# Late expert tiles: the store and the DMA transpose of half the inner layer move from SP's queue to ScalarE's, and the transpose moves behind turn_h

## The chip, the core and the metric

The kernel runs on one core of one Trainium2 chip. The metric is the device time of one execution in microseconds. The core has five engines that run their own instruction streams in order: TensorE (PE; PEld are its weight loads), VectorE (DVE), ScalarE (ACT), GpSimd (POOL) and SyncE (SP), which in this kernel issues nearly all plain DMA transfers.

## The reference

Attention with rotary embedding over 4 batches, 8 heads, 576 tokens and head size 64 is followed by a mixture of 8 experts. A token takes a fresh expert when its local gate is under 0.5, otherwise it keeps that of the token before it.

```python
x = attn_out.transpose(0, 2, 1, 3).reshape(B, S, 512)
...
for s in range(S):
    e = fresh_e if s == 0 or local_gate[b, s] < 0.5 else prev_e
    h = np.maximum(x[b, s] @ w1[e], 0.0)       # 512 -> 1024, the inner layer
    out[b, s] = p[e] * (h @ w2[e])             # 1024 -> 512
```

## The kernel before

The first part (to about 280 us) is attention and routing. The tokens are then sorted by expert into tiles of 128, and the experts run tile by tile: tiles 0 to 5 are the early ones, 6 to 18 the late ones, and tile 18 is the last. Float32 products are made of three passes over split numbers (a high part and the rest, `PASSES`). The change touches the late tiles alone, and there only tiles 6 to 17 (`by_dma`).

For each tile `first_product` makes the inner layer `h` in PSUM: 4 steps of 6 matmuls. `second_product` of the tile before it runs in between: 4 steps of 6 matmuls on the transposed, split inner layer `hs` (8 blocks of 128). A step of it reads two of the eight blocks of `hs`; the first two steps read blocks 0 to 3, the last two blocks 4 to 7.

The inner layer has to be transposed between the two products. Of tiles 6 to 17 the first half goes through TensorE: ScalarE applies the Relu (L943), `turn_h` transposes four blocks (L967), ScalarE copies the high part (L303) and VectorE makes the rest (L307). The second half goes through DRAM: VectorE copies it out of PSUM as two 16-bit planes (L942), a DMA stores the planes to `inner_d` (L944), and a DMA transpose brings them back as `ht` (L951, in `land_h`). One tile later `split_landed` makes the high part with Relu on ScalarE (L957) and the rest on VectorE (L958). The DMA transpose waits for the store's landing.

The weights of a tile are 8 chunks of 1024 columns, in four pairs A, B, C and D. They are loaded to the buffer `stage` by SP and split into a high part and the rest by `split_w`. Both happen only where the tile's expert differs from that of the tile before it; for late tiles each engine jumps over its share otherwise (L884 is that branch). For a late tile, of the splits of A (chunks 0 and 1) the high parts are on POOL (L877) and the rests on VectorE (L878). Of B, C and D, ScalarE makes the high parts of chunks 2, 5, 6 and 7 (L875), and POOL both parts of chunk 4. `load_pair(t + 1, c)` (L838) follows each split in SP's order. Where experts change from one tile to the next can be seen in the profile by the L875, L877 and L878 work: the new weights of tiles 11, 13 and 18 are split in late tiles, A and B during the tile before, C and D during the tile itself.

The order on every engine is the order in which the program is written; no scheduler moves anything in the late tiles. It is a string with one letter for each act:

```python
TILE = "ffAgffHfxBTssshsCDs"
```

`f` is a step of the first product, the fifth `f` takes the inner layer out of PSUM (L942, L943) and issues the store (L944). `x` transposes the next tile's tokens, `A` to `D` are the weight splits, `s` is a step of the second product, and the fifth `s` scales its result on ScalarE (`os`, L981) and issues POOL's scatter to the output (L982). `g` is POOL's gather of token rows (L908), `h` is `turn_h`, `T` is `land_h` and `H` is `split_landed` of the tile before.

Of the kernel before, what the change touches and what calls it, by code (L numbers as in the profile page):

```python
# [46 lines left out]
SPREAD_LAST = 127  # L47

TILE_EARLY = ("ffAffsfxBssgCsshD", "ffAffxfsBsCsgsshD", "fffAffxBssChsgssD", "ffAfffxBsssshsCDg", "ffAfffBsssxsshCgD", "fffxAffsBssgssChD")
TILE = "ffAgffHfxBTssshsCDs"  # L50
TILE_LAST = "ffxAffHfssBsChsDss"
PULL = 3
PE_LAG = 2
# [84 lines left out]
def tile_attention_moe(ctx, tc, qk, v, tabs, turn, consts, tri, wg, wts, out):  # L138
    nc = tc.nc
    pe, act, dve, pool, sp = nc.tensor, nc.scalar, nc.vector, nc.gpsimd, nc.sync  # L140
# [31 lines left out]
    inner_d = [dram.tile([P, 2, 512], U16, name=f"inner_{i}") for i in range(2)]  # L172
# [754 lines left out]
    def first_product(t):  # L927
        ps = ps_s.tile([P, 2, 512], F32, tag="s", name=f"h_{t}")
        for k in range(4):
            w = w_t.pop((t, k))  # L930
            for n, (x, y) in enumerate(PASSES):
                for c in range(2):
                    pe.matmul(ps[:, c], xs_t[t][:, x, k], w[y][:, c * 512:(c + 1) * 512],  # L933
                              start=(k == 0 and n == 0), stop=(k == 3 and n == 2))
            yield k
        h = ej_p.tile([P, 2, S], F32, tag="ej", name=f"hr_{t}").rearrange("p a s -> p (a s)")[:, 0:1024]
        h_t[t] = h
        if not by_dma(t):
            act.activation(h, ps.rearrange("p c n -> p (c n)"), AF.Relu)
            return  # L940
        planes = h[:, 512:].bitcast(U16).rearrange("p (l n) -> p l n", l=2)
        dve.tensor_copy(planes, ps[:, 1].bitcast(U16).rearrange("p (n l) -> p l n", l=2))  # L942
        act.activation(h[:, 0:512], ps[:, 0], AF.Relu)  # L943
        sp.dma_start(inner_d[t % 2], planes)  # L944

    def by_dma(t):
        return KE <= t < LAST

    def land_h(t):
        x = pk_p.tile([P, S], F32, tag="pk", name=f"ht_{t}")[:, 0:512]  # L950
        sp.dma_start_transpose(  # L951
            x.bitcast(U16).rearrange("p (k n) -> p k n", k=4), inner_d[t % 2].rearrange("t l n -> (t l) n"))
        landed[t] = x.rearrange("p (k n) -> p k n", k=4)

# [16 lines left out]
    def second_product(t):  # L971
        ps = ps_t.tile([P, 512], F32, tag="t", name=f"o_{t}")
        for k in range(8):
            w = w_t[t, 4 + k // 2]
            for n, (x, y) in enumerate(PASSES):
                pe.matmul(ps, hs_t[t][:, x, k], w[y][:, (k % 2) * 512:(k % 2 + 1) * 512],  # L976
                          start=(k == 0 and n == 0), stop=(k == 7 and n == 2))
            if k % 2 == 1:
                yield k
        o = et_p.tile([P, S], F32, tag="et", name=f"os_{t}")  # L980
        act.activation(o[:, 0:DM], ps, AF.Copy, scale=x_t[t][:, DM:DM + 1])  # L981
        done = pool.indirect_dma_start(  # L982
            out=outf, out_offset=bass.IndirectOffsetOnAxis(ap=sidx[:, t:t + 1], axis=0),
            in_=o[:, 0:DM], in_offset=None, bounds_check=NT - 1, oob_is_err=False)

        tc.declare_no_dep(done.ins, group="rows out", reason="rows of their own")
        tc.add_to_no_dep_group("rows out", done.ins)
# [3 lines left out]
    def experts_phase():  # L991
        for t in range(LAST + 1):
            first = first_product(t)
            second = second_product(t - 1) if t > 0 else iter(())
            for c in TILE_LAST if t == LAST else TILE if t >= KE else TILE_EARLY[t]:
                if c == "f":
# [10 lines left out]
                elif c == "s":  # L1007
                    if next(second, None) is not None:
                        yield t
                elif c == "x" and t < LAST:  # L1010
                    turn_x(t + 1)
                elif c in "AB" and t < LAST:
                    split_w(t + 1, "AB".index(c))
                elif c in "CD" and t > 0:
                    split_w(t, 2 + "CD".index(c))
                elif c == "h":
                    turn_h(t)
                    yield t + 1
                elif c == "T":
                    land_h(t)  # L1020
                elif c == "H" and by_dma(t - 1):
                    split_landed(t - 1)
                elif c == "g":
                    if t == 0:
                        gather(4)
                        gather(5)
                    elif KE < t + 2 <= LAST:
                        gather(t + 2)
# [3 lines left out]
    def rest_phase():  # L1032

        nl = nc.values_load_multi_w_load_instructions(meta[0:1, 60:61], min_val=U_LATE - 1, max_val=NLATE)[1][0]  # L1034

        def rest(t):
            with tc.If(nl > t - KE):
                expert_of(t)
                for k in range(8):
                    load_w(t, k)  # L1040
                regs.pop(t)
                gather(t)
                turn_x(t)
                for c in range(4):
                    split_w(t, c)
                list(first_product(t))
                turn_h(t)
                list(second_product(t))
                if t + 1 < NTILE:
                    rest(t + 1)  # L1050

        if LAST + 1 < NTILE:
            rest(LAST + 1)
# [294 lines left out]
```

## Time and profile before

| | |
|---|---|
| median of 3 runs | 549.62 us (549.24 to 551.68) |
| the profiled execution | 548.69 us, its span 546.8 us |
| PE busy | 520.2 us, 95% of the span |
| VectorE busy | 401.7 us, 73% |
| ScalarE busy | 334.1 us, 61% |
| POOL busy | 327.6 us, 60% |
| stores L944, DMA transposes L951 | 12 and 12, all on SP |

The span runs from the first to the last instruction. A row of the timeline gives the start in us, the time in us, engine, line, operation, what it writes and reads, the count, and in brackets how long the engine was idle before it and what ended that. "ACTq" and the like are the sequencers of the engines, with which branches and DMA issues are done. Rows of matmuls are modelled, so that neighbours can overlap a little.

### The profile page before, as it was taken

How to read it: one execution, taken by the hardware profiler on the slowest of the kernel's cores; microseconds unless marked ns; L12 is line 12 of the kernel's file. 1: busy time of each engine (PE TensorE's matmuls, PEld its weight loads, DVE VectorE, ACT ScalarE, POOL GpSimd, SP SyncE). 2: the span in 40 equal slices, each digit the busy share in tenths (PEclk: the TensorE clock that was granted, in tenths of full speed). 3: DMA queues.
4: the chain of work that ended last, by engine and by line, in shares of the span. 5: the costliest groups of instructions: out<-in, count | busy, mean ns of one | idle time of the engine just before them, and what ended most of it. 6: DMA issues, size and time to landing. Idle time of an engine off the chain costs nothing. (4 is left out here: it accounts for less than half of the span.)

```text
span 546.8 us, 10672 instructions
## 1 busy us (share of the span) xinstructions
PE 520.2 (95%) x3280; PEld 459.5 (84%) x3281; DVE 401.7 (73%) x736; ACT 334.1 (61%) x754; POOL 327.6 (60%) x243
## 2 busy tenths in 40 slices
PE   7989999999999999998999999999999998999992
PEld 4788999999999999997888788887888886888871
DVE  6898999999999999999999845348422757522650
ACT  2899889888998999987667523351421333422340
POOL 2997989888777988986698202355412453411341
PEclk9999999999999999999999999999999999999997
DMA  8759688776887787885288214553437394635350
GB/s 249 297 123 230 180 242 236 175 200 184 229 229 180 210 223 203 214 220 146 34 201 233 70 27 167 166 220 120 171 98 241 107 352 138 200 102 183 117 184 25
DMA packets 62024, 97.35 MB, mean 178 GB/s; under 512 B 27969, under 2 KB 38209, under 8 KB 59010
## 3 DMA queue, kind: packets, MB, share of 16 engines
q1 hardware_dynamic: 58914, 86.84, 55.4%
q0 software_dynamic: 3040, 9.71, 5.7%
q8 instruction: 28, 0.46, 0.3%
q14 instruction: 42, 0.34, 0.2%
HBM read 76.98 MB, written 12.86 MB: 164 GB/s over the span
## 5 line engine op out<-in xcount | busy, mean ns | idle before, releaser
L976 PE MATMUL o<-w,hs 128*128 128x512 f32 x456 | 113.5, 398 | 2.2 <-DVE hs L307 1.0
L272 DVE TENSOR_REDUCE mn<-s 128x1 f32<-128x576 f32 x144 | 107.3, 746 | 3.6 <-PE s L267 2.2
L933 PE MATMUL h<-w,xs 128*128 128x512 f32 x444 | 106.1, 392 | 0.9 <-DVE xs L307 0.6
L289 ACT ACTIVATE e<-s,mn 128x576 f32<-128x576 f32 x128 | 95.2, 744 | 18.7 <-DVE mn L272 15.4
L267 PE MATMUL s<-m,qst 128*128 128x288 f32 x512 | 97.4, 310 | 5.4 <-ACT e L289 3.2
L307 DVE TENSOR_TENSOR ptl<-tm,pth 128x512 fp32r<-128x512 f32 x139 | 95.1, 684 | 6.5 <-ACT pth L303 4.1
L976 PEld LDWEIGHTS o<-w,hs 128*128 128x128 f32 x456 | 83.0, 188 | 19.8 <-DVE hs L958 1.4
L982 POOL DMA_INDIRECT out_dram<-os,sidx x19 | 23.5, 1238 | 126.8 <-ACT os L981 79.7
L933 PEld LDWEIGHTS h<-w,xs 128*128 128x128 f32 x444 | 82.6, 188 | 19.1 <-DVE w L878 1.1
L303 ACT CAST pth<-tm 128x512 fp32r<-128x512 f32 x139 | 80.8, 582 | 12.3 <-PE tm L325 11.2
L267 PEld LDWEIGHTS s<-m,qst 128*128 128x128 f32 x512 | 74.7, 188 | 12.2 <-ACT e L289 6.2
L325 PE MATMUL tm<-wid,e 128*128 128x128 f32 x512 | 77.0, 272 | 1.3 <-ACT e L289 0.5
L361 PE MATMUL pv<-pth,v 128*128 128x288 f32 x256 | 76.4, 314 | 0.4 <-DVE ptl L307 0.2
L361 PE MATMUL pv<-ptl,v 128*128 128x288 f32 x256 | 76.5, 314 | 0.0
L196 POOL TENSOR_TENSOR stage<-stage 128x1152 f32<-128x1152 f32 x26 | 69.0, 2665 | 10.5 <-DMA stage<-in_qk_dram 10.5
L878 DVE TENSOR_TENSOR w<-stage,w 128x1024 fp32r<-128x1024 f32 x41 | 56.8, 1424 | 22.3 <-POOL w L877 13.9
L325 PEld LDWEIGHTS tm<-wid,e 128*128 128x128 f32 x512 | 62.0, 140 | 2.2 <-DVE ptl L307 1.0
L361 PEld LDWEIGHTS pv<-pth,v 128*128 128x128 f32 x256 | 48.2, 188 | 2.8 <-DVE ptl L307 0.9
L361 PEld LDWEIGHTS pv<-ptl,v 128*128 128x128 f32 x256 | 48.3, 189 | 0.0
L943 ACT ACTIVATE hr<-h 128x512 f32<-128x512 f32 x12 | 7.2, 599 | 50.5 <-DVE hr L942 50.5
L307 DVE TENSOR_TENSOR hs<-th,hs 128x512 fp32r<-128x512 f32 x26 | 17.4, 687 | 27.3 <-ACTq L884 17.0
L197 POOL TENSOR_TENSOR stage<-stage 128x576 f32<-128x576 f32 x26 | 36.9, 1430 | 0.2
(195 smaller groups left out, 815.4 us busy)
## 6 DMA issues: line engine op xcount, KB each, us to landing
stage<-in_wts_dram SPq DMA_DIRECT2D x70, 512.0 KB
stage<-in_qk_dram SPq DMA_DIRECT2D x13, 1152.0 KB
stage<-in_wts_dram SPq DMA_DIRECT2D x9, 1024.0 KB
qst<-xq SPq DMA_DIRECT2D x56, 128.0 KB
stage<-in_v_dram SPq DMA_DIRECT2D x16, 320.0 KB
m<-xq SPq DMA_DIRECT2D x14, 288.0 KB
m<-xk SPq DMA_DIRECT2D x14, 288.0 KB
m<-xq SPq DMA_DIRECT2D x14, 256.0 KB
```

Of the source, the lines that this page charges most:

```text
L196: engine.tensor_tensor(x, x, tab[:, 2 * f:2 * f + 2], op=ALU.mult)
L197: engine.tensor_tensor(rr[:, f], x[:, 0], x[:, 1], op=ALU.add)
L267: pe.matmul(st[:, h, lo:hi], lhs, keys[:, k0:k0 + hi - lo], start=(n == 0), stop=(n == len(parts_) - 1))
L272: dve.tensor_reduce(mn, s_t[g][:, :, 0:HALF], axis=AX.XY, op=ALU.min)
L289: act.activation(dst.rearrange("p (h s) -> p h s", h=2), s_t.pop(g)[:, :, 0:HALF], AF.Exp, bias=mn, scale=-1.0, accum_out=sums[:, col:col ...
L303: act.copy(hi, src)
L307: dve.tensor_tensor(lo, src, hi.bitcast(F32), op=ALU.subtract)
L325: pe.transpose(ps[:, k], src[:, k * P:(k + 1) * P], ident)
L361: pe.matmul(pv_t[p, u], lhs.rearrange("p c d -> p (c d)"), rhs, start=(n == 0), stop=(n == 9))
L878: (pool if k in on_pool else dve).tensor_tensor(lo, src, hi.bitcast(F32), op=ALU.subtract)
L933: pe.matmul(ps[:, c], xs_t[t][:, x, k], w[y][:, c * 512:(c + 1) * 512], start=(k == 0 and n == 0), stop=(k == 3 and n == 2))
L976: pe.matmul(ps, hs_t[t][:, x, k], w[y][:, (k % 2) * 512:(k % 2 + 1) * 512], start=(k == 0 and n == 0), stop=(k == 7 and n == 2))
```

## The change

ScalarE's queue issues the store and the DMA transpose instead of SP's. In the order of a late tile the letter `T` (the DMA transpose) moves from behind `B` to behind `h`, ahead of the step of the second product that precedes `C` and `D`.

```diff
-TILE = "ffAgffHfxBTssshsCDs"
+TILE = "ffAgffHfxBssshTsCDs"
...
         act.activation(h[:, 0:512], ps[:, 0], AF.Relu)
-        sp.dma_start(inner_d[t % 2], planes)
+        act.dma_start(inner_d[t % 2], planes)
...
     def land_h(t):
         x = pk_p.tile([P, S], F32, tag="pk", name=f"ht_{t}")[:, 0:512]
-        sp.dma_start_transpose(
+        act.dma_start_transpose(
             x.bitcast(U16).rearrange("p (k n) -> p k n", k=4), inner_d[t % 2].rearrange("t l n -> (t l) n"))
```

## Rows read from the trace of the kernel before

**Rows 1.** Busy times in three stretches: tile 11, tile 12, the end.

```profile
core 0: us, PE busy (x) PEld busy (x) DVE busy (x) ACT busy (x) POOL busy (x), PEclk, DMA share, GB/s
432.51:444.34 11.83, 11.83 (x57) 9.80 (x56) 5.50 (x7) 3.53 (x6) 5.92 (x4) 1.00 0.84 288
444.34:458.75 14.41, 12.66 (x58) 9.56 (x57) 10.67 (x10) 6.03 (x9) 6.77 (x5) 1.00 0.58 201
...
518.03:537.00 18.97, 17.70 (x81) 14.09 (x79) 9.63 (x9) 7.18 (x10) 6.87 (x4) 1.00 0.44 151
```

**Rows 2.** Timeline of PE: two of the four rows with idle time from 380 us on.

```profile
455.10 1.20 PE L976 MATMUL o<-w,hs 128*128 128x512 f32 x4 [1.01 <-DVE hs L958]
...
531.47 5.28 PE L976 MATMUL o<-w,hs 128*128 128x512 f32 x22 [1.01 <-DVE hs L307]
```

**Rows 3.** Timeline of VectorE in tile 12.

```profile
450.36 3.19 DVE L878 TENSOR_TENSOR w<-stage,w 128x1024 fp32r<-128x1024 f32 x2 [2.09 <-POOL w L877]
453.47 1.57 DVE L958 SCALAR_TENSOR_TENSOR hs<-ht,hs 128x512 fp32r<-128x512 f32 x1
454.96 1.21 DVE L942 COPY hr<-h 128x1024 uint16<-128x1024 uint16 x1
```

**Rows 4.** Timeline of POOL from tile 11 to tile 12.

```profile
447.50 1.73 POOL L982 DMA_INDIRECT out_dram<-os,sidx  x1 [3.52 <-ACT os L981]
449.27 2.06 POOL L877 TENSOR_SCALAR w<-stage 128x1024 fp32r<-128x1024 f32 x2
```

**Rows 5.** Timeline of ScalarE: tile 9, and tile 11 into tile 12.

```profile
419.57 0.59 ACT L303 CAST hs<-th 128x512 fp32r<-128x512 f32 x1 [2.71 <-PE th L967]
420.90 0.69 ACT L981 ACTIVATE os<-o,x 128x512 f32<-128x512 f32 x1 [0.74 <-PE o L976]
...
443.21 0.59 ACT L303 CAST hs<-th 128x512 fp32r<-128x512 f32 x1 [2.71 <-PE th L967]
443.69 2.94 ACT L875 CAST w<-stage 128x1024 fp32r<-128x1024 f32 x3
446.54 0.69 ACT L981 ACTIVATE os<-o,x 128x512 f32<-128x512 f32 x1
452.67 0.63 ACT L957 ACTIVATE hs<-ht 128x512 fp32r<-128x512 f32 x1 [5.45 <-DMA ht<-inner]
```

**Rows 6.** Timeline of SP's queue: tile 8, and tiles 10 to 11.

```profile
403.97 0.36 SPq L944 DMA_DIRECT2D inner<-hr  x1
406.06 1.26 SPq L951 DMA_TRANSPOSE ht<-inner  x1
...
435.14 4.18 SPq L838 DMA_DIRECT2D stage<-in_wts_dram  x4
439.62 0.48 SPq L944 DMA_DIRECT2D inner<-hr  x1
...
448.61 1.27 SPq L951 DMA_TRANSPOSE ht<-inner  x1
```

**Rows 7.** Waits of SP's queue, 375 to 545 us: total, times, longest.

```profile
SPq L951 <- DMA inner<-hr: 26.4, 10, 6.6
...
SPq L838 <- DVEq L884: 9.3, 8, 1.5
```

**Rows 8.** Instructions on the tile inner: ns min, median and max of an issue.

```profile
L944 SPq DMA_DIRECT2D inner<-hr x12: 337/354/478, 381.9 to 515.3; - x12
L951 SPq DMA_TRANSPOSE ht<-inner x12: 1244/1266/1366, 387.3 to 517.4; - x12
```

**Rows 9.** DMA queues from 440 to 441 us: packets, MB, share of 16 engines.

```profile
q1 hardware_dynamic: 57, 0.23, 57.5%
q0 software_dynamic: 46, 0.18, 44.6%
```

**Rows 10.** DMA issues from 399 to 411 us: the gather's median time to landing.

```profile
x<-rows_d,gidx POOLq DMA_INDIRECT x1, 3.8
```

**Rows 11.** DMA issues from 435 to 447 us: the same for tile 11's gather.

```profile
x<-rows_d,gidx POOLq DMA_INDIRECT x1, 7.3
```

## The prediction

> **What bounds the kernel now.** I read the stretches by tile first, then PE's timeline, and then went back from each of PE's waits, engine by engine. PE is busy 95% of the span, and in a late tile without trouble it never stops: tile 11 takes 11.83 us and PE is busy in all of them [rows 1]. From 380 us on PE has only four rows with idle time: three in tile 12 and one in tile 18 [rows 2]. Tile 12 takes 14.41 us, 2.58 more than tile 11 [rows 1]. So whatever the change saves can come to no more than 2.58 us there and 1.01 us in tile 18, about 3.6 us or 0.65% in all. What it costs has no such bound. A delay on ScalarE in a quiet tile is lost in slack, but one that reaches these places goes to the end one to one.
>
> What is late in tile 12 is not the transposed half by itself. The matmul of 455.10 waits for VectorE's rest of that half (L958), and this began at 453.47, with no idle time before it, directly behind VectorE's rests of split A, 450.36 to 453.55 [rows 2, 3]. Those waited 2.09 us for POOL's high parts (L877, from 449.27), which stand directly behind POOL's scatter of 447.50, which had waited 3.52 us for ScalarE's `os` [rows 3, 4]. `os` ran at 446.54, directly behind ScalarE's three weight casts of C and D, and these began at 443.69, directly behind the copy of `turn_h` at 443.21 [rows 5]. That is an unbroken chain: the copy of `turn_h`, three casts, `os`, the scatter, split A on POOL, split A on VectorE, L958, PE. The DMA transpose landed at about 452.7, where ScalarE's L957 had waited 5.45 us for it [rows 5], but L957 was done by 453.30, and VectorE was not free before 453.5. Both arms arrive almost together, and the longer one begins on ScalarE.
>
> **What is removed.** Twelve stores and twelve transposes leave SP. On SP an issue costs 0.354 and 1.266 us (medians), and SP waited 26.4 us in ten places for a store to land, at worst 6.6 us, in tile 11 [rows 7, 8]. There the store stood behind four weight loads in one queue: issued at 439.62, transposed at 448.61 [rows 6]. This looks like the thing to gain. But who would get the time? The weight loads behind it on SP wait for VectorE's branches, 9.3 us in eight places [rows 7], since the buffer is free only when the split before has been read. These releases do not move, so I cost the relief of SP at nothing. Of the transposed half, an earlier landing gains nothing in tile 12 either, as the other arm ends at 453.5 all the same. If that arm were gone, L957 would be worth up to 2.58 us.
>
> **What is added to ScalarE.** The store comes behind the Relu of the first half: 0.35 us of issue, then `x` and `B`. It pushes the copy of the next tile's tokens, and in a tile with a split B its cast and `turn_h`'s copy too; these have slack in quiet tiles, where ScalarE is busy under a third of the time. The transpose comes behind the copy of `turn_h`. It has to wait until the store has landed, and then costs 1.27 us of issue [rows 8]. Everything behind it on ScalarE waits with it: the branches and casts of C and D, `os` and through it POOL's scatter, gather and next split, and then L957.
>
> In a quiet tile the store lands 2.1 us after its issue (403.97 to 406.06) [rows 6], before the copy of `turn_h`, so that the transpose need not wait. In tile 9, if its issue begins with the copy at 419.57 and runs 1.27 us beside it, it ends at 420.84, before `os` at 420.90. If it begins only when the copy ends (420.16), `os` is 0.53 us late [rows 5]. This matters where a split A follows, in tiles 10 and 17: between 0 and 0.53 us each. I take 0.1 each, 0.2 in sum. In the others the transposed half comes about a microsecond later than now, and it has several microseconds until the third step of the next second product; nothing is lost.
>
> Tile 11 is the place that decides. The casts of C and D began 0.48 us into the copy, at 443.69 [rows 5]. Now the transpose is ahead of them. It can begin at 443.3 at the earliest, and if the store has landed by then, the casts begin at 444.55, 0.85 us later. When does the store land? It is issued at about 439.7. Alone it would land 2.1 us later, at 441.8. But weight loads are in flight. From 440 to 441 us SP's queue (q1) moved 57 packets and POOL's (q0, the gather) 46 [rows 9]: two queues that have work take turns, almost one to one, although q1's work was issued first. The 103 packets of that microsecond on 16 engines are 0.155 us each. The store is 128 rows of 2 KB, 8 packets on each engine. If each waits for one packet of the weights, that adds 1.2 us; if also for one of the gather, 2.5 us. So the store lands between 443.0 and 444.3, the transpose begins between 443.3 and 444.3, and the casts are late by 0.85 to 1.9 us. I take 1.3.
>
> The Trainium skill ("DMA: Bandwidth & Descriptors", section "Queues, rings and completion order") says that SP and ACT each own a row of rings on the same DMA engines, and that an engine goes round the rows packet by packet. The 57 to 46 of POOL's and SP's queues agree [rows 9]; no row here shows ACT's queue. By that rule the sum is the one below.
>
> The bounds: at the least 0, if the issue keeps ScalarE's sequencer busy, but the casts' chain makes it up. A gain in this chain I exclude, as nothing is taken from it. At the most, the store loses what the gather lost beside the same loads: 7.3 us to landing in tile 11 against 3.8 in tile 8 [rows 10, 11], so 3.5 us. It then lands at 445.3, the transpose ends at 446.6, and the casts are 2.9 us late.
>
> In tiles 6 and 13 a store also meets loads and casts of C and D stand behind it, but no split A follows in the next tile, and PE has no idle time there. I take 0, at most 0.5 for both.
>
> Tile 18: PE waited 1.01 us for VectorE at 531.47 [rows 2]. Its weights for C and D are loaded when VectorE has passed tile 17's `turn_h`. That is behind split B's rest, which waits for ScalarE's cast of chunk 2, now behind a store's issue: 0.35 us late [rows 8]. I take 0.3; bounds 0 and 0.5, with the transpose's packets near the loads.
>
> **The sum.** 1.3 + 0.2 + 0.3 = 1.8 us. At the most 2.9 + 1.1 + 0.5 + 0.5 = 5.0, at the least 0. Against the profiled execution, 548.69 us, this is 550.5. That execution is 0.93 us below the median of the runs, 549.62, so for the median 551.4.
>
> **The rivals.**
>
> Nothing is lost. ScalarE's issues run beside its arithmetic, or the chain of tile 11 absorbs 0.85 us. For it speaks that ScalarE waits often and long, 5.45 us in one place [rows 5]. Against it, that the chain from 443.21 to 455.10 has no idle time between its members. Time: 549.6.
>
> A wait that moves to a worse place. If the store on ScalarE's queue is not served beside SP's backlog but lands when it does now, shortly before 448.61 [rows 6], ScalarE stands still from 443.7 to 449.9: casts, `os`, scatter and split A are 6.2 us late, and tile 12 with them. With 0.5 elsewhere that is 549.6 + 6.7 = 556.3. It decides from where the store lands after about 444.8: then the delay with 0.5 elsewhere passes 2.75 us. For it speaks that SP's four issues took 4.18 us, about three times the 0.35 of a lone one [rows 6, 8], so that issues can be held up. Against it, that POOL's gather went past the backlog [rows 9]. The same page of the Trainium skill (section "Issuing engines are not separate DMA queues") says that another issuing engine saves only the issue time on the sequencer; taken at its word, the store gains no place in the line, and this case follows. Its condition is that the turns of [rows 9] do not hold for ScalarE's queue.
>
> Faster. The store of tile 11 lands 5 us earlier, the transposed half is there before 450, and with no transfer in the way split A is done by 451.2. Then tile 12 runs like tile 11, 2.58 us less [rows 1]: 547.0; with tile 18's 1.01 too, 546.0. For it speaks the wait of 5.45 us. Against it, that split A hangs on `os`, which can only come later. It decides only if VectorE's rests of split A end over 2 us earlier than 453.55.
>
> **How the numbers follow.** The forecast has 0.62, nothing lost 0.16, the wait on ScalarE 0.13, faster 0.09. About 0.5% (2.75 us) is what a measurement here can tell from no change. Slower by more: the 0.13 and about a seventh of the forecast's 0.62 (sums over 2.75), 0.22. Faster by more: only if both waits of PE go, 0.03. The rest, 0.75, is within 0.5%. The range reaches from 548.8, which takes in nothing lost with the scatter of the runs, to 554.6, the upper sum on the median. Left out are the wait of 6.7 us and most of the gain, about 0.2. The forecast's own range is 550.4 to 554.6.
>
> **What would show it.** Right: tile 11's transpose on ScalarE's queue issued between 443.3 and 444.4 and taking about 1.27 us, the three casts behind it starting near 445, split A on VectorE near 451.6, and tile 12 at 15.3 to 16.3 us; the quiet tiles still 11.8; SP's loads where they were. Wrong: a store that takes over 6 us to land in tile 11 and ScalarE silent until 449; PE idle in tiles 10 and 17; or a tile 12 under 14 us, because split A does not hang on `os` as I read it. The clock should not matter: it was 1.00, the upper level of 2.4 GHz, in tile 12 with its 1.75 us of idle PE [rows 1].

## The result and the profile after

The changed kernel takes 557.32 us (median of 6 runs, 556.22 to 557.84) against 549.25 us: 1.0142 times as long by the means of the runs, 95% interval 1.0118 to 1.0167. The forecast was 551.4 us with a range to 554.6. The profiled execution has a span of 554.8 us against 546.8, so 8.0 us have to be found.

Four stretches of the changed kernel, tiles 7, 10, 12 and 17 from one first product to the next; the columns are those of [rows 1]:

```profile
385.36:398.25 12.89, 12.32 (x58) 9.64 (x56) 6.72 (x8) 5.71 (x8) 3.58 (x3) 1.00 0.38 112
421.93:434.26 12.33, 12.08 (x57) 9.72 (x56) 7.18 (x7) 3.83 (x6) 6.07 (x5) 1.00 0.39 126
446.08:465.72 19.64, 13.46 (x58) 10.65 (x57) 11.18 (x10) 6.55 (x9) 6.78 (x5) 0.83 0.46 160
513.17:525.48 12.31, 12.09 (x58) 9.72 (x57) 7.13 (x7) 3.82 (x6) 4.26 (x4) 1.00 0.45 103
```

Tile 7 of the kernel before:

```profile
385.26:397.07 11.81, 11.81 (x57) 9.79 (x56) 6.75 (x8) 5.20 (x8) 3.44 (x3) 1.00 0.41 135
```

Tile 12 took 14.41 us before and takes 19.64: 5.23 us of the 8.0. Tile 7 took 11.81 and takes 12.89 (+1.08), tile 10 11.81 and 12.33 (+0.52), tile 17 11.87 and 12.31 (+0.44). Some 0.2 us come with tile 18; the rest lies ahead of the late tiles and behind PE's last matmul.

PE's waits in the changed kernel from 375 us on (total, times, longest), the answer to [rows 2]:

```profile
PE o L976 <- DVE hs L958: 6.2, 1, 6.2
PE o L976 <- DVE hs L307: 1.2, 1, 1.2
PE th L967 <- ACT hr L943: 1.0, 3, 0.6
```

The one long wait is for the same instruction as before, VectorE's L958 in tile 12. The chain behind it has the same members as in [rows 3 to 5]. ScalarE of the changed kernel in tile 11 and into tile 12, in order of time:

```profile
441.18 0.35 ACTq L944 DMA_DIRECT2D inner<-hr  x1
...
444.94 0.59 ACT L303 CAST hs<-th 128x512 fp32r<-128x512 f32 x1 [2.69 <-PE th L967]
448.56 1.27 ACTq L951 DMA_TRANSPOSE ht<-inner  x1
450.15 2.95 ACT L875 CAST w<-stage 128x1024 fp32r<-128x1024 f32 x3 [4.62 <-DMA stage<-in_wts_dram]
453.00 0.68 ACT L981 ACTIVATE os<-o,x 128x512 f32<-128x512 f32 x1
453.58 0.62 ACT L957 ACTIVATE hs<-ht 128x512 fp32r<-128x512 f32 x1
```

The casts of C and D began 0.48 us after the start of the copy of `turn_h` [rows 5] and now begin 5.21 us after it, 4.73 us later. Between them the transpose stands: it is issued at 448.56, 7.38 us after the store, and takes 1.27 us. The bracket of the casts names a weight load, the event that came last by the profile; the order on ScalarE shows that the casts could not run before the transpose was issued, and in the run without the wait, below, where it is issued earlier, they run earlier. L957 now follows `os` directly: the transposed half is no longer waited for. Then POOL and VectorE, the same links as in [rows 3, 4]:

```profile
453.96 1.74 POOL L982 DMA_INDIRECT out_dram<-os,sidx  x1 [7.95 <-ACT os L981]
455.72 2.06 POOL L877 TENSOR_SCALAR w<-stage 128x1024 fp32r<-128x1024 f32 x2
```

```profile
456.81 3.18 DVE L878 TENSOR_TENSOR w<-stage,w 128x1024 fp32r<-128x1024 f32 x2 [2.09 <-POOL w L877]
459.92 1.57 DVE L958 SCALAR_TENSOR_TENSOR hs<-ht,hs 128x512 fp32r<-128x512 f32 x1
```

VectorE's rests of split A began 6.02 us into tile 12 (444.34 to 450.36, [rows 1, 3]) and now begin 10.73 us into it: 4.71 us later. So the delay of the casts came through the whole chain undiminished. The other 0.5 us of tile 12 is PE's clock. Two stretches in that tile, columns as above:

```profile
458.00:460.00 2.00, 0.00 (x0) 0.00 (x0) 2.00 (x3) 0.00 (x0) 1.98 (x2) 0.50 0.00 0
...
462.00:464.00 2.00, 2.00 (x7) 1.40 (x7) 0.86 (x2) 1.34 (x3) 0.00 (x0) 0.50 0.26 95
```

PE's last matmul before the wait ended at 455.4. The granted clock was 0.50 at 458, the lower level of 1.2 GHz, and still 0.50 when the work came back: the four matmuls released at 461.55 took 2.07 us, where the four of [rows 2] took 1.20.

SP's side shows where the relief went (SP's waits, total, times, longest):

```profile
SPq L838 <- DVEq L884: 67.2, 8, 16.3
```

SP waits as often as before for VectorE's branches, eight times, but 67.2 us instead of 9.3 [rows 7]: the time that it no longer spends on the store and the transpose it spends on the next branch.

### The profile page after: what moved, and what is told of

Its sections match the earlier page's. It is cut to its first block, busy times and chain, and to the rows that moved or that the text cites. A ratio compares the mean times of both kernels' runs of the same rounds, so it can differ in the third digit from the quotient of the medians.

```text
span 554.8 us, 10676 instructions
## 1 busy us (share of the span) xinstructions
PE 523.3 (94%) x3280; PEld 460.7 (83%) x3281; DVE 402.0 (72%) x736; ACT 333.8 (60%) x754; POOL 327.0 (59%) x243
## 5 line engine op out<-in xcount | busy, mean ns | idle before, releaser
L875 ACT CAST w<-stage 128x1024 fp32r<-128x1024 f32 x28 | 28.1, 1052 | 13.8 <-issue 6.6
```

## The experiments

The theories in the first four runs are called "wait" (the transpose's wait for the store, ahead of C, D and `os` on ScalarE), "issue" (ScalarE's time for the issues) and "queue" (ScalarE's DMA queue is served worse). Each ratio is of means, to the kernel before in the same series.

**The store alone on ScalarE's queue.** The transpose stays on SP, at its old place.

```diff
-        sp.dma_start(inner_d[t % 2], planes)
+        act.dma_start(inner_d[t % 2], planes)
```

> The kernel before with one part of the change: ScalarE issues the store, SP the transpose, at its old place. Theory 'wait' (the transpose's wait for the store, ahead of the casts of C and D and of os on ScalarE, is the loss): ScalarE gets 0.35 us an issue and no wait, SP waits for tile 11's store until about 448.5 as before, tile 12 stays within 0.5 us of 14.4 us, and the time is 549 to 550. Rival 'issue' (the time of the issues on ScalarE is the loss): 0.35 of the 1.62 us an issue pair, so about 551. Rival 'queue' (ScalarE's DMA queue is served worse than SP's, and what comes late through it is the loss): the transposed half of tile 11 lands later than 452.7 us, and the time is 551 to 555.

Measured: 549.33 us against 548.93, ratio 1.0007 (0.9989 to 1.0025). ScalarE's and SP's rows in tile 11:

```profile
440.36 0.34 ACTq L944 DMA_DIRECT2D inner<-hr  x1
...
444.08 0.59 ACT L303 CAST hs<-th 128x512 fp32r<-128x512 f32 x1 [2.69 <-PE th L967]
444.56 2.95 ACT L875 CAST w<-stage 128x1024 fp32r<-128x1024 f32 x3
...
451.46 0.63 ACT L957 ACTIVATE hs<-ht 128x512 fp32r<-128x512 f32 x1 [3.37 <-DMA ht<-inner]
```

```profile
447.68 13.34 SPq L951 DMA_TRANSPOSE ht<-inner  x2
```

The store took about as long as in the changed kernel (440.36 to 447.68, 7.3 us), but it was SP that waited. The casts are back at 0.48 us behind the copy. The row of SP merges two transposes; its start is tile 11's. The first product of tile 12 began at 445.21, so L957 came 6.25 us into the tile instead of 8.33, and tile 12 still took 14.41 us (445.21 to 459.62): an earlier transposed half gains nothing while split A sets the end.

**The transpose alone on ScalarE's queue.** The changed kernel with the store back on SP.

```diff
-        act.dma_start(inner_d[t % 2], planes)
+        sp.dma_start(inner_d[t % 2], planes)
```

> The changed kernel with the store back on SP's queue; ScalarE issues only the transpose, behind the copy of turn_h. 'Wait': the store now stands behind SP's weight loads and lands in tile 11 between 448.5 and 449.5, ScalarE stands still as in the changed kernel or up to 1 us longer, and the time is 557 to 558.5. 'Issue': 556.5. 'Queue': the store is back on the good queue, and the time falls to 550 to 552.

Measured: 557.17 us, ratio 1.0157 (1.014 to 1.0174). ScalarE in tile 11:

```profile
449.15 1.24 ACTq L951 DMA_TRANSPOSE ht<-inner  x1
450.72 2.94 ACT L875 CAST w<-stage 128x1024 fp32r<-128x1024 f32 x3 [5.38 <-issue]
```

PE waited 6.56 us for L958 in tile 12. The store was issued at 441.85 on SP and let the transpose go 7.3 us later, as on ScalarE's queue. All of the loss is there with the transpose alone, none of it with the store alone. "Queue" falls.

**The transpose behind `os`.** Both issues on ScalarE, the transpose at the end of the string.

```diff
-TILE = "ffAgffHfxBssshTsCDs"
+TILE = "ffAgffHfxBssshsCDsT"
```

> The changed kernel with the transpose at the end of the tile's string, behind C, D and os on ScalarE; both issues stay on ScalarE. 'Wait': nothing on the chain to split A waits for the store any more; tile 12 is back to 14.0 to 14.9 us, tile 11's transpose is issued near 448.5 us and tile 12's L957 is about where it was before; 549 to 550.5. 'Issue': the same twelve times 1.62 us on ScalarE, so 555 to 557. 'Queue': 553 to 557, as the transposed half comes later still in quiet tiles.

Measured: 549.35 us, ratio 1.0013 (1.0000 to 1.0027). ScalarE in tile 11:

```profile
442.78 0.59 ACT L303 CAST hs<-th 128x512 fp32r<-128x512 f32 x1 [2.73 <-PE th L967]
443.27 2.95 ACT L875 CAST w<-stage 128x1024 fp32r<-128x1024 f32 x3
446.12 0.68 ACT L981 ACTIVATE os<-o,x 128x512 f32<-128x512 f32 x1
446.50 1.27 ACTq L951 DMA_TRANSPOSE ht<-inner  x1
```

The same twelve pairs of issues on ScalarE cost nothing that can be measured, once what is urgent stands ahead of them; the store has landed by the time `os` runs. Tile 12 is at 14.40 us. "Issue" falls as the main cause.

**No wait, same place.** The transpose reads what the tile before stored.

```diff
-            x.bitcast(U16).rearrange("p (k n) -> p k n", k=4), inner_d[t % 2].rearrange("t l n -> (t l) n"))
+            x.bitcast(U16).rearrange("p (k n) -> p k n", k=4), inner_d[max(t - 1, KE) % 2].rearrange("t l n -> (t l) n"))
```

> The changed kernel, but the transpose of a tile reads the DRAM buffer that the tile before it stored (tile 6 its own), so from tile 7 on it need not wait for a store just issued; the second half of the inner layer is then that of the tile before. Issue time and place are unchanged. 'Wait': in tile 11 the transpose is issued right behind the start of turn_h's copy, the casts of C and D start 0.9 to 1.3 us later than in the kernel before, tile 12 takes 15.3 to 15.8 us, tile 7 still loses its 1.1 us, and the time is 551 to 552.5. 'Issue': unchanged, 556 to 557.5. 'Queue': 555 or more, as the transposes still go through ScalarE's queue beside the loads.

Measured: 552.24 us, ratio 1.0057 (1.004 to 1.0074). ScalarE in tile 11, and a stretch of tile 12:

```profile
445.59 0.59 ACT L303 CAST hs<-th 128x512 fp32r<-128x512 f32 x1 [2.73 <-PE th L967]
445.67 1.30 ACTq L951 DMA_TRANSPOSE ht<-inner  x1
447.29 2.95 ACT L875 CAST w<-stage 128x1024 fp32r<-128x1024 f32 x3 [1.11 <-POOL w L878]
```

```profile
462.00:464.00 2.00, 2.00 (x6) 1.52 (x6) 2.00 (x2) 0.32 (x1) 0.00 (x0) 0.50 0.45 77
```

This is the price of the issue alone: the casts start 1.70 us behind the copy instead of 0.48, 1.22 us late. Tile 12 took 17.10 us, 2.69 more than before, which I had put at 0.9 to 1.4: the clock fell here too, to 0.50 behind a PE wait of 2.69 us, and six matmuls of the second product took 2.91 us instead of 1.64. Tile 6 still read its own store; tile 7 lost 1.57 us. So without the wait some 3 us of the loss remain (552.24 against 548.93), and the wait itself is the other 5 of the 8.

**`os` ahead of C and D**, tried to shorten the chain in the kernel before.

```diff
-TILE = "ffAgffHfxBTssshsCDs"
+TILE = "ffAgffHfxBTssshssCD"
```

> The kernel before (both issues on SP, transpose behind B) with one move in the order of a late tile: the last step of the second product, that is os on ScalarE and the scatter on POOL, ahead of C and D instead of behind them. If the chain in tile 12 is as read (turn_h's copy, three casts, os, scatter, split A on POOL, split A on VectorE, L958), os of tile 11 runs near 444.5 us instead of 446.5, the scatter near 445.3, split A on VectorE near 448.5 to 449.5; L958 then waits for the transposed half, which lands at 452.7 as before, and tile 12 takes 13.2 to 13.9 us instead of 14.4; the time is 548.2 to 549.0 against 549.25. If split A hangs on something else (its weights, VectorE's splits of C and D), tile 12 stays at 14.4 us and the time is the same.

Measured: 557.70 us, ratio 1.0168 (1.0147 to 1.0189). The same order with the store on ScalarE's queue as well:

> As the last, with the store on ScalarE's queue and the transpose on SP's. If the store on ScalarE's queue really lands near the same time as on SP's (about 448 us in tile 11), there is nothing over the last kernel: 548.2 to 549.2. If a queue of its own lets the store by, the transposed half of tile 11 lands 2 to 4 us earlier, tile 12 takes 12 to 12.6 us, and the time is 547 to 547.8.

Measured: 557.41 us, ratio 1.0162 (1.0139 to 1.0184). Both expectations were wrong. POOL of the first of the two:

```profile
448.17 1.01 POOL L982 DMA_INDIRECT out_dram<-os,sidx  x1 [8.98 <-ACT os L981]
...
450.38 3.23 POOL L878 TENSOR_TENSOR w<-stage,w 128x1024 fp32r<-128x1024 f32 x1
```

With `os` goes POOL's scatter, which waits for it, and now it stands ahead of POOL's split of chunk 4 (449.22 to 453.61). In the old order POOL did that split before 444.0, while it would have waited for `os`. Split A follows it, from 453.58; in the kernel before it began at 449.27 [rows 4]. It is the fault of the change once more, on another engine: a wait moved ahead of work that had filled its time.

**Finer weight loads beside the store.** The changed kernel with the 1 MB pairs loaded as two transfers (rows of 4 KB), and, cut likewise once more, all of them with rows of 2 KB. Their sources have one line less and one more, so the line numbers behind the cut differ by one.

```diff
-                for k, n in ((6, 1), (7, 1)) if c == 3 else ((2 * c, 2),):
-                    to = stage[:, k * 1024:(k + n) * 1024] if k < 7 else staged(7)
-                    sp.dma_start(to, wts[bass.ds(e, 1), :, k * 1024:(k + n) * 1024])
+                for k in (2 * c, 2 * c + 1):
+                    sp.dma_start(staged(k), wts[bass.ds(e, 1), :, k * 1024:(k + 1) * 1024])
```

> The changed kernel with the late weight loads cut finer: pairs A, B and C of a late tile as two loads of 512 KB, rows of 4 KB instead of 8 KB; D was so already. In the changed kernel tile 11's store was issued at 441.2, its first packets moved about 3 us later and its last at 448.0, beside weight packets of 4 and then 8 KB. If turns go by packets, the store's share beside the loads grows in the stretch with 8 KB packets: it lands about 1 us earlier, ScalarE's wait is 1 us shorter, 555.5 to 556.5. If the store lands when the bytes ahead of it are done, whatever the packets, nothing changes: 557 within 0.6.

> The same with rows of 2 KB for all late weight loads (quarters of a pair, 256 KB each). If turns go by packets and the 3 us before the store's first packet are a fixed count of packets already handed to the DMA engines, the store starts 1 to 1.5 us after its issue and is through within 2 us: it lands 3 to 4 us earlier than in the changed kernel, tile 12 shrinks from 19.6 to 15.5 to 16.5 us, and the time is 553 to 554.5. If the lag is a count of bytes, the start stays at 3 us, only the turns are quicker, and the time is 555 to 556. If neither plays a part, 557 within 0.6; more issues on SP (0.35 us each) may cost up to 0.5 us of their own.

Measured: 554.04 us, ratio 1.0103 (1.0059 to 1.0146), with 4 KB, below the 555.5 to 556.5 expected, from four runs between 551.65 and 557.22; 562.98 us, ratio 1.0265 (1.024 to 1.0289), with 2 KB, above every value expected. With 4 KB the store of tile 11 was issued at 441.84 and the transpose at 447.73: 5.9 us instead of 7.4. Tile 12 took 18.07 us, and tile 18's wait was gone (17.71 us to PE's end instead of 18.92). With 2 KB ScalarE could not issue the store:

```profile
442.31 0.60 ACT L944 ACTIVATE hr<-h 128x512 f32<-128x512 f32 x1 [2.77 <-DVE hr L943]
448.13 0.36 ACTq L945 DMA_DIRECT2D inner<-hr  x1
448.59 0.59 ACT L303 CAST xs<-tx 128x512 fp32r<-128x512 f32 x1 [5.67 <-DMA stage<-in_wts_dram]
```

In the other runs with the store on ScalarE's queue it goes out with the Relu, at most 0.1 us behind its start. Here it came 5.8 us later. No expectation had that. The bracket names the reason, the landing of a weight load: in this program the store's issue waits for a semaphore that SP's weight loads use too, and the load before it on that semaphore, issued at 444.64, landed at 448.11, 0.02 us ahead of the store's issue. The same happened in tile 13 (481.70 and 481.72). So this run has a wait of its own on ScalarE, and its time does not tell what turns with 2 KB packets are worth.

**Split A later, to take L958 out of the chain.** On the kernel before: A, with its load, behind the transpose.

```diff
-TILE = "ffAgffHfxBTssshsCDs"
+TILE = "ffgffHfxTABssshsCDs"
```

> The kernel before (both issues on SP), with split A and the load that follows it moved from the second step of a late tile to behind the DMA transpose: x, T, A, B. By the theory, tile 12 loses its 2.6 us because L958 stands behind split A on VectorE, and split A behind os; and the store of tile 11 is late because A's load of 1 MB stands ahead of it on SP. With the move, L958 no longer waits for split A, the store lands near 444.5 us, the transposed half near 448, and tile 12 takes 11.8 to 12.3 us; the last tile keeps its 1.0 us. 546.3 to 547.5 against 549.2. Rival: split A is needed for the next tile's first product and comes too late there (PE waits for VectorE's w in L933, 1 to 3 us in tiles 11, 13 and 18), and the time is 549 to 552.

Measured: 546.59 us against 549.11, ratio 0.9944 (0.9922 to 0.9967). Tile 12, and its transpose on SP, issued 5.4 us after the store (440.45), with the loads of A and B behind it:

```profile
445.37:457.18 11.81, 11.81 (x57) 9.79 (x56) 9.18 (x9) 4.60 (x7) 4.97 (x5) 1.00 0.79 265
```

```profile
445.84 1.27 SPq L951 DMA_TRANSPOSE ht<-inner  x1
```

Tiles 7 to 17 all take 11.81 us now. The same order with the change's engines:

```diff
-TILE = "ffAgffHfxBssshTsCDs"
+TILE = "ffgffHfxABssshTsCDs"
```

> The changed kernel (both issues on ScalarE, transpose behind turn_h) with split A and its load behind x. ScalarE still waits for the store in tile 11, but behind it there is no split A that L958 needs; and A's load is issued behind the store. If the loss of the change is the delay of split A through os, most of it goes: tile 12 12 to 13 us, 547 to 549. If the standstill of ScalarE costs by itself (the casts of C and D late for the second product, L957 behind os), 552 to 556. If the store starts to move only when the loads issued before it are done, ScalarE's wait in tile 11 ends 2 to 3 us earlier than in the changed kernel, as C and D alone are ahead of it.

Measured: 553.14 us, ratio 1.0066 (1.0039 to 1.0093). This is the second case, the standstill that costs by itself (552 to 556), not the first (547 to 549). PE's two largest waits (total, times, longest), and VectorE in tile 12:

```profile
PE th L967 <- ACT hr L943: 2.3, 4, 0.6
PE o L976 <- POOL w L878: 2.0, 1, 2.0
```

```profile
450.82 3.50 DVE L878 TENSOR_TENSOR w<-stage,w 128x1024 fp32r<-128x1024 f32 x3 [4.17 <-ACT w L875]
454.81 0.69 DVE L958 SCALAR_TENSOR_TENSOR hs<-ht,hs 128x512 fp32r<-128x512 f32 x1 [0.49 <-ACT hs L957]
```

The long wait of tile 12 is gone (the 2.0 us are in tile 18), but ScalarE still stood until 448.20, so the casts of C and D are late, VectorE's rests of them end at 454.3, and L958, L942, the Relu and TensorE's transposes come after. Tile 12 takes 12.74 us, tile 13 13.20, and three more tiles 12.7 to 12.8; the standstill has more than one way to PE. The transpose went out 6.5 us after the store, 0.9 us sooner than in the changed kernel, not the 2 to 3 us sooner of a store that starts when the loads issued before it are done. The third order kept both issues on SP, with the transpose behind A and B:

```diff
-TILE = "ffAgffHfxBTssshsCDs"
+TILE = "ffgffHfxABTssshsCDs"
```

> As the first of these three, but with the transpose behind B on SP: x, A, B, T. The loads of A and B are then ahead of the transpose on SP's queue and the transposed half of tile 11 lands near 451 to 452.5 us. If only split A's place mattered, 546.3 to 547.5 as well; if the landing matters once split A is out of the way, tile 12 takes 12.3 to 13.5 us, and the time is 547 to 548.3.

Measured: 550.24 us, ratio 1.0024 (1.0008 to 1.0041), over both expected values. ScalarE in tile 12, and PE's clock in tile 18 (columns as above):

```profile
452.73 0.63 ACT L957 ACTIVATE hs<-ht 128x512 fp32r<-128x512 f32 x1 [4.19 <-DMA ht<-inner]
```

```profile
534.00:536.00 2.00, 2.00 (x5) 1.61 (x6) 2.00 (x2) 0.00 (x0) 1.81 (x1) 0.50 0.02 8
```

Tile 12 takes 13.61 us (445.65 to 459.26): L957 waits for the transposed half, 7.1 us into the tile instead of 3.8 with the transpose ahead of A and B. With split A out of the way its landing does count. Tile 18 waits 2.03 us for POOL's split, and behind this wait the granted clock was 0.50: the 23 matmuls that follow took 7.12 us, where the same 23 took 5.52 at 1.00 in the run before. Why POOL's split came late in this order was not followed.

**The late split A on SP, with the 4 KB rows** (line numbers one lower, as there).

> The version with split A and its load behind the transpose on SP (546.6 us), with the late pairs A, B and C loaded as two transfers of 512 KB (rows of 4 KB) instead of one of 1 MB. Of the changed kernel this cut took 1.2 us from tile 18, because chunk 4 lands alone and POOL's split of it is over earlier, so that VectorE's split of chunk 5 runs less beside it; PE's last wait there went. If that holds here, tile 18's wait of 1.18 us goes, and the time is 545 to 546. If the four more issues on SP hold up a store or a transpose, a late tile grows by 0.5 to 1 us and the time is 546.5 to 547.5.

Measured: 544.88 us against 549.89, ratio 0.9918 (0.9893 to 0.9944): faster than both kernels. Whether the 4 KB rows add to the late split A is not settled by the times, as this interval overlaps the one of the late split A alone (0.9922 to 0.9967, in another series). In the trace the last tile's wait for VectorE is gone. PE's waits from 375 us on:

```profile
PE th L966 <- ACT hr L942: 0.4, 1, 0.4
PE h L932 <- DVE w L877: 0.3, 1, 0.3
```

## Why the prediction was wrong

What held: the bound (PE, with four waits in the late tiles), the chain of tile 12 from `turn_h`'s copy over casts, `os`, scatter and split A to L958, and that a delay at its start reaches PE one to one (4.73 us in, 4.71 out). The relief of SP gained nothing, nor did an earlier transposed half (549.33 us with the store alone moved). The price of an issue on ScalarE was that on SP (0.353 and 1.270 us, medians), and the issue alone put the casts 1.22 us late where 0.85 was the least. Tiles 10 and 17 lost 0.52 and 0.44 us, near their bound of 0.53; I had taken 0.1 each, hoping that the issue runs beside the copy. It does begin beside it (in tile 9 at 420.87, the copy at 420.80), but `os` came at 422.75, 0.6 us after the issue's end.

The step that failed is the landing of tile 11's store. I took 1.2 to 2.5 us over a lone store's 2.1, from the turns that POOL's and SP's queues take [rows 9], and 3.5 at the most from the gather's [rows 10, 11]. Measured were 5.3 us over it (7.38 in all). ScalarE stands still until the store lands, which is the wait of the second rival, given 0.13; the casts are late by 4.7 us where that rival had 6.2 and the forecast 1.3. Almost all of the 5.3 us is in two parts of about the same size. SP's and POOL's queues from 441 to 444.4 us, and SP's and ScalarE's (q10) from 444.4 to 448.4 (packets, MB, share):

```profile
q1 hardware_dynamic: 200, 0.78, 59.7%
q0 software_dynamic: 156, 0.52, 39.7%
```

```profile
q1 hardware_dynamic: 248, 1.44, 86.1%
q10 hardware_dynamic: 144, 0.26, 17.0%
```

In the first stretch no packet of ScalarE's queue moved: the store's first packet came 3.5 us behind its issue, where that of a lone store (tile 10) came 0.85 us behind it. This term was put at nothing. In the second the turns are there: from 445 to 447 us q1 moved 122 packets and q10 113. The store's packets took 3.2 us instead of 0.7, 2.4 us more, which is the upper end of the 1.2 to 2.5; q1's packets were 5.8 KB in the mean and not the 4 KB of [rows 9], as the rows of the 1 MB loads are 8 KB. So the rule of the Trainium skill ("DMA: Bandwidth & Descriptors", section "Queues, rings and completion order") that the prediction cites agrees with that stretch; what I drew from it, that the store would soon be through, does not follow. With 4 KB rows both parts were shorter, 2.8 and 2.5 us, and the wait 1.5 us shorter.

The reading of [rows 9] hid the first part. I wrote that the turns are taken "although q1's work was issued first"; but the four loads are one merged row in [rows 6], and singly they were issued at 435.14, 436.14, 436.82 and 438.97, each in 0.33 to 0.36 us. The gather went out ahead of three of them, in the kernel before:

```profile
435.55 1.04 POOL L908 DMA_INDIRECT x<-rows_d,gidx  x1 [0.30 <-PE h L933]
```

From 437 to 439.6 us that trace has packets of SP's queue alone:

```profile
q1 hardware_dynamic: 139, 0.99, 92.1%
```

The gather's first packet moved at 439.70, 4.2 us after its instruction began, against 2.0 us in tile 8 (399.56 to 401.60). So the gather was no proof that a later transfer goes past a backlog; it had been held too.

The prediction cites the same page of the Trainium skill a second time, from the section "Issuing engines are not separate DMA queues", for the rival in which another queue gains the store no place in the line. Two pairs of runs bear on it: with the transpose on ScalarE the store took 7.3 us on SP's queue and 7.4 on ScalarE's, which agrees; with the transpose on SP it took 9.0 us on SP's queue (439.62 to 448.61 [rows 6]) and 7.3 on ScalarE's, so there the other queue gained the store 1.7 us.

Two more terms were missing. Tile 7 lost 1.08 us, as the store of tile 6 also came late (the transpose went out at 387.51, 6.6 us after the store, and the casts at 389.06 instead of 384.61); with the transpose off ScalarE, or behind `os`, tile 7 was back at 11.81. I had put tiles 6 and 13 at 0.5 at the most, as no split A follows there. And the clock: "should not matter" was judged by 1.75 us of idle PE in several pieces. It fell in tile 12 of the changed kernel, with its wait of 6.2 us, and cost 0.5 us there.

## What to carry to other kernels

A DMA that must wait for another DMA belongs on an engine whose queue holds nothing urgent behind it. Its issue cost the same on SP and on ScalarE; its wait is paid by whatever stands behind it in program order, here three casts, a result, a scatter and the next tile's weights. Before a wait is moved, follow each instruction behind it to whoever waits for that one, on every engine: moving `os` forward failed on POOL in the same way. When an engine seems to lose time in a wait, find what it would do otherwise; SP's 26.4 us were worth nothing, while the order of one weight split and its load was worth 2.5 us. And a merged row of the timeline does not tell the order of issues on two engines: before one transfer is taken to have passed another, read the single issues and the first packets.

## What the runs showed of the hardware

With split A early and rows of 8 KB, a store of 256 KB beside the weight loads of tile 11 took 7.3 to 7.6 us on ScalarE's queue and 7.3 to 9.0 on SP's, from its issue to that of the transpose that waited for it; in a quiet tile 2.1. On ScalarE's queue its first packet moved 3.5 us (changed kernel) and 3.9 us (store alone) behind its issue, and the rest then took turns with the loads for 3.2 and 2.7 us. On SP's queue, behind the loads, the first packet moved after 5.9 us (kernel before) and 5.7 us (transpose alone), and the rest took 2.6 and 1.0 us. So a queue of its own let the store begin sooner and move more slowly. What holds it for the first 3.5 us is not settled. It was less beside shorter rows: 2.8 us with 4 KB, 1.5 with 2 KB, though that store went out 5.8 us late.

PE's granted clock was 0.50 (1.2 GHz) behind PE waits of 6.2 us (changed kernel), 2.7 us (older data), 2.03 us (tile 18 of the last order with late split A) and 1.93 us (2 KB rows, at 447.4: the 24 matmuls behind it took 7.31 us instead of 5.63). Behind the 2.00 us of late split A with the issues on ScalarE it stayed at 1.00. In the changed kernel the first matmuls behind the wait ran at 0.50; with the older data the first four still took 1.19 us and the later ones were slow. Where the clock fell, the wait cost more than its length: 0.5 us more in the changed kernel's tile 12, 1.6 us in that tile 18.
